# Cell 7 of an mLSTM, the last of its first full chunk, computed in turned form like the cells after it

## The chip, the core and the metric

The kernel runs on one core of one Trainium2 chip. Its engines work side by side and meet through semaphores: PE (TensorE, matrix products), DVE (VectorE), ACT (ScalarE), POOL (GpSimd) and SP (SyncE, which here issues nearly all transfers, in the order of its queue). The metric is the device time of one execution in microseconds (us). Three runs of the kernel before took 536.65, 540.45 and 540.67, the median is 540.45.

## The reference, cut to what matters

There are 4 batches and 8 heads, 768 tokens, head dimension 40. For every batch and head an mLSTM runs over the tokens:

```
m_new  = max(f + m, i);  fs = exp(f + m - m_new);  is = exp(i - m_new)
C      = fs * C + is * outer(v, k)
n      = fs * n + is * k
y      = sigmoid(o_gate) * (C q) / max(|n . q|, 1)
```

The result, 3072 tokens of 320 values (8 heads by 40), goes through a feed-forward block with 2048 inner units, `h = x @ w_in; out = (h * cos(h)) @ w_out`. Everything is float32.

## The kernel before

**Cells.** The sequence is cut in 6 chunks of 128 tokens. A cell is one chunk of one batch, all 8 heads; cell n = 4c + b is batch b of chunk c, so there are 24. Within a chunk the recurrence is written as products: the scores k q of all pairs of tokens (`scores`, L440), weighted with exponentials of the gates (`weigh`, L450, into the tile E), times the values; and what the chunks before left in the state `st[b]`, times q. The state is then faded and added to (`fade` L560, `seam` L569 and `state` L596). The value tile and the state carry one column more, from which n . q comes.

**Two forms of a cell.** Cells below `TURNED` (L70, here 8) take the plain form. q and k come as tokens by (head, dimension). PE transposes them (`turn`, L421, eight transposes for the four head pairs of q and k), ACT copies them out of PSUM (`turn_out`, L432). `values_kept` (L455) multiplies q with the state, and `values` (L466) the weights with the values; both give tokens by dimensions. `normalize` (L525) on DVE scales the state's part, adds, divides and applies the output gate. In `seam` PE transposes the result back in three blocks (L576), and `seam_out` (L590) copies it on ACT into `xT`, the input of the feed-forward block (dimensions by tokens).

Cells from `TURNED` on take the turned form. q and k are loaded in blocks (L319 to L325, eight transfers of 32 rows each), such that `turn_blocks` (L406) can turn them with DVE, one instruction for each of q and k (L412); the second half of that function scales q with the gate G, which `load_G` (L331) has spread over the rows (L415), and turns the output gate, loaded in blocks as well (L304 to L306), in two instructions (L419). `values_turned` (L475) computes dimensions by tokens at once: 16 products of the state with the scaled q (L484), 16 of the values with the weights (L490), each float32 product as two instructions. `normalize_turned` (L493) needs no transposes on PE: it works in place, writes the first 32 dimensions of each head into `xT` (L516), and sends the last 8 through a scratch in DRAM, two writes (L520) and two reads into `xT` (L523).

**Order.** The whole program is written out by hand, and every engine works through its own queue in that order. `first_cells` (L768) does the cells of chunk 0 and the first loads. Then `both_parts(c, b)` (L904) takes a quarter of the feed-forward block of chunk c together with cell n = 4(c + 1) + b, so that cell 7 lies in both_parts(0, 3) and its preparation at the end of both_parts(0, 2). A part runs: the up products of one eighth (class `Up`, L621 and L624 on PE), scores, then on ACT and DVE the steps near (L629), rest (L632), sin (L637) and gate (L641); the down products of the eighth before (`down`, L744, products at L754 while c = 0); the values and the normalizing of the cell; the second eighth likewise, with seam, state and weigh_k; its down products; and last the turning of the next cell. The PSUM pools are small: two banks for up products, two for the cells (`ps_a`), four for the down products.

While c = 0, the float weights are still being put together from raw bits: each piece is loaded into a tile `bits` (L129 for w_in, L170 for w_out, 8 pieces of w_out with three buffers), prepared on ACT (`parts`, L132), and joined on DVE and POOL (`join`, L143; POOL's addition is L149). Piece p of w_out serves down(c, p). The load of piece p + 3 stands in SP's queue where piece p is joined (`out_join`, L899), and it waits there until the buffer is read. Two pieces are joined in each part of c = 0, the second one after the turning of the next cell (L1014 to L1020). The output gates of chunk c + 2 are loaded in part (c, 2) (L975) and go through the sigmoid on ACT in part (c, 3) (L939); the weights E of cell n + 1 are prepared in part n (`decay_by_bias`, L383, while c = 0).

Of the kernel before, what the change touches and what calls it, by code (L numbers as in the profile page):

```python
# [29 lines left out]
def kernel(  # L30
# [22 lines left out]
    B, H, S, D = q.shape  # L53
# [13 lines left out]
    DA, DL, T4 = 32, 8, 4  # L67
    assert DM - NK * 128 == 64 and NF % 4 == 0 and DA + DL == D
    NB = 4
    TURNED = 2 * B  # L70
    SPREAD = (0, 1)

    const = ctx.enter_context(tc.tile_pool(name="const", bufs=1))
# [218 lines left out]
    def load_o(c, bs=range(B)):  # L292
        if c not in sig:
            sig[c] = p2.tile([128, B * DM + LO], FP, name="o", tag="o")
            if c > 1:
                nc.gpsimd.memset(sig[c][:, B * DM:], 0.0)
        for b in bs:
            o = sig[c][:, ts(b, DM)]
            if c * B < TURNED:
                nc.sync.dma_start(out=o.rearrange("t (h d) -> t h d", h=H),  # L300
                                  in_=o_gate[b, :, ts(c, C)].rearrange("h t d -> t h d"))
                continue

            for k4 in range(HP):  # L304
                nc.sync.dma_start(out=o[ts(k4, 32)].rearrange("r (i x) -> r i x", i=2),
                                  in_=o_gate[b, ts(k4, 2), ts(c, C)].rearrange("i (r x) d -> r i (x d)", x=T4))  # L306
# [5 lines left out]
    def blocks(n):  # L312
        return [qbs[n % 2 + i].rearrange("r (p x) -> r p x", p=HP) for i in (0, 2)]

    def load(n, which="qkv"):
        c, b = divmod(n, B)
        i = n % NB
        if n >= TURNED:
            for dst, src in zip(blocks(n), (q, k)):  # L319
# [42 lines left out]
    def psum_o():  # L362
        return ps_o.tile([128, HP, C], FP, name="pm", tag="o")
# [33 lines left out]
    def psum(n):  # L397

        return (ps_o, "o") if n < B and n % 2 == 1 else (ps_a, "a")
# [6 lines left out]
    def turn_blocks(n):  # L406


        c, b = divmod(n, B)
        qkT[n] = [p2.tile([128, HP, C], FP, name=f"t{i}", tag=f"t{i}") for i in range(2)]  # L410
        for dst, src in zip(qkT[n], blocks(n)):
            nc.vector.transpose(out=dst.rearrange("r p (t x) -> r p x t", x=T4),  # L412
                                in_=src.rearrange("r p (x d) -> r p x d", x=T4)[:, :, :, 0:32])
        qgs[n] = rooms[0][:, 0:HP * C].rearrange("r (p t) -> r p t", p=HP)
        nc.vector.tensor_tensor(out=qgs[n], in0=qkT[n][0], in1=Gs[n], op=OP.mult)  # L415
        oTs[n] = rooms[4][:, 0:4 * C].rearrange("r (i h t) -> r i h t", i=2, h=2)
        for half, lo in enumerate((0, LO)):
            o = sig[c][:, b * DM + lo:(b + 1) * DM + lo].rearrange("r (i x d) -> r i x d", i=2, x=T4)
            nc.vector.transpose(out=oTs[n][:, :, half].rearrange("r i (t x) -> r i x t", x=T4), in_=o[:, :, :, 0:32])  # L419
# [20 lines left out]
    def scores(n):  # L440
        pool, tag = psum(n)
        qT, kT = qkT[n]
        ps = [pool.tile([128, HP, C], FP, name="ps", tag=tag) for _ in range(2)]
        for p in range(HP):
            for j in range(2):
                r = slice(64 * j, 64 * j + (64 if n < TURNED else D))
                nc.tensor.matmul(ps[j][:, p], kT[r, p], qT[r, p], start=True, stop=True)  # L447
        pss[n] = ps

    def weigh(n):  # L450
        for j in range(2):
            w = Es[n].rearrange("p (a j) t -> p a j t", j=2)[:, :, j]
            nc.vector.tensor_tensor(out=w, in0=pss[n][j], in1=w, op=OP.mult)  # L453

    def values_kept(n):  # L455

        pool, tag = (ps_o, "o") if n == B else psum(n)
        heads_of[n] = None
        if n >= B:
            pq = pool.tile([128, H, D1], FP, name="pq", tag=tag)  # L460
            for p in range(HP):
                nc.tensor.matmul(pq[:, 2 * p:2 * p + 2].rearrange("p j d -> p (j d)"), qkT[n][0][:, p],
                                 st[n % B][:, p].rearrange("p j d -> p (j d)"), start=True, stop=True)
            heads_of[n] = pq
# [104 lines left out]
    def seam(n):  # L569

        pool, tag = psum(n)
        if n < TURNED:

# [78 lines left out]
    def parted(c):  # L652
        return c > 0
# [18 lines left out]
    def sums(c, f2):  # L672

        if not parted(c):
            return
        S = p2.tile([128, 4, C], FP, name="sg", tag="wt")
        A11, A21, A12, A22 = (gs[c, 2 * f2 + e][:, ts(b, C)] for e in range(2) for b in range(2))
        for i, (x, y, op) in enumerate(((A21, A22, OP.add), (S[:, 0], A11, OP.subtract),
                                        (A11, A21, OP.subtract), (A12, S[:, 1], OP.subtract))):
            nc.gpsimd.tensor_tensor(out=S[:, i], in0=x, in1=y, op=op)  # L680
        sg[c, f2] = S
# [81 lines left out]
    def warm(k, bank=None):  # L763

        for _ in range(k):
            nc.tensor.matmul(bank or pw, nil, nil.unsqueeze(1).to_broadcast([128, HP, 128]), start=True, stop=True)
# [128 lines left out]
    def out_parts():  # L895
        p, piece = outs.pop(0)
        return p, parts(*piece)
# [6 lines left out]
    def both_parts(c, b):  # L904

        n = (c + 1) * B + b
        cell = n < N  # L910
        begin = c == b == 0
        more = cell and n + 1 < N
        f2 = 2 * b
        up = Up(c, f2, cell_after_first if begin else None)
        if cell:
            scores(n)
            if begin:
                values_kept(n)

                warm(6, psum_o())  # L920
        for e in range(2):
            up.near(e)
        if begin:
            weigh(n)
        for e in range(2):
            up.rest(e)
        if cell and not begin:
            weigh(n)
        if begin or more and c > 0:
            decay_exponents(n + 1)  # L930
        for e in range(2):
            up.sin(e)
            up.gate(e)
        sums(c, f2)
        if c == 0 and b == 1:
            sigmoid(1, slice(1, B))
        if begin:
            sigmoid(1, slice(0, 1))
        if b == B - 1 and c + 2 < NC:  # L939
            sigmoid(c + 2)  # L940
        h = ()
        if c == 0 and not begin:
            out_join(*out_parts())
        if pieces:
            h = parts(*pieces.pop(0))
        rest = None
        if b == 0 and c > 0 and parted(c - 1):
            rest = down(c - 1, NF // 2 - 1)
        if begin or more and c > 0:
            decay(n + 1)  # L950
        elif more:
            decay_by_bias(n + 1)
        if f2 > 0:
            down(c, f2 - 1)
        elif rest:
            rest()
        elif c > 0:
            down(c - 1, NF // 2 - 1)
        if cell:
            if n + 2 < N:  # L960
                load(n + 2)
            if n < TURNED:
                if not begin:
                    values_kept(n)
                values(n)
                normalize(n)
            else:
                values_turned(n)
            if h:
                join(*h)  # L970
            if TURNED <= n + 2 < N:
                load_G(n + 2)
            if n + 3 < N:
                load_E(n + 3)
            if b == B - 2 and c + 2 < NC:  # L975
                load_o(c + 2)
            if n >= TURNED:
                normalize_turned(n)
            fade(n)
        h = ()  # L980
        sin_next()
        if pieces:
            h = parts(*pieces.pop(0))
        up = Up(c, f2 + 1)
        if cell:
            seam(n)
        for e in range(2):
            up.near(e)
        for e in range(2):
            up.rest(e)  # L990
        if cell and n < TURNED:
            seam_out(n)
        if h:
            join(*h)
        if cell:
            state(n)
        for e in range(2):
            up.sin(e)
            up.gate(e)
        sums(c, f2 + 1)  # L1000
        if more:
            weigh_k(n + 1)
        if c == 0 and b == B - 1 or c == 1 and b < B - 1:
            two_differences(c * (2 * b + 2))
        if pieces:
            join(*parts(*pieces.pop(0)))
        down(c, f2)
        if pieces:
            join(*parts(*pieces.pop(0)))
        if c == 0:  # L1010
            if b + 2 < B:
                pieces.extend(weights_in(b + 2))
            h = out_parts()
        if more and n + 1 < TURNED:  # L1014
            turn(n + 1)
            turn_out(n + 1, c > 0)
        elif more:
            turn_blocks(n + 1)
        if c == 0:
            out_join(*h)  # L1020

# [37 lines left out]
```

## Time and profile before

| what | us |
|---|---|
| median of three runs (536.65, 540.45, 540.67) | 540.45 |
| the profiled execution, its time | 537.82 |
| the profiled execution, its span (first to last instruction) | 536.1 |
| PE busy in the span | 524.8 |
| DVE, ACT, POOL busy | 365.7, 261.6, 168.0 |
| both_parts(0, 2), by its up products on PE | 83.42 to 106.78 |
| both_parts(0, 3) | 106.78 to 129.44 |
| both_parts(1, 0), first products | 129.44 |

Times inside the profile count from the span's start. A line of a timeline gives start, length, engine, source line and operation, the tile written and those read, the shape and how many instructions are merged; in brackets the idle time before it and what ended that. The chain of waits is followed back from the last instruction, at each step to what released it. "SPq L170" is the issue of a transfer by SP's queue at line 170. The granted clock of PE is 1.0 throughout.

### The profile page before, as it was taken

The numbers are of one execution on the slowest core, as the hardware profiler recorded it, in microseconds if no ns is written. First come the engines' busy times: TensorE is split into PE (matmuls) and PEld (weight loads), VectorE is DVE, ScalarE is ACT, GpSimd is POOL, SyncE is SP. The second block draws the span as 40 slices with busy tenths as digits, with TensorE's granted clock in tenths as the row PEclk, the third lists the DMA queues.
The fourth block names the chain that finished last, engine by engine and source line by source line (L and its number), as shares of the span: only waits on it lengthen the run. The fifth ranks groups of instructions, "written<-read, shape, count | busy, mean of one in ns | idle before, by whom it ended". The sixth has DMA issues, their size and how long they took to land.

```text
span 536.1 us, 9942 instructions
## 1 busy us (share of the span) xinstructions
PE 524.8 (98%) x3634; PEld 332.6 (62%) x3634; DVE 365.7 (68%) x727; ACT 261.6 (49%) x416; POOL 168.0 (31%) x304
## 2 busy tenths in 40 slices
PE   9888999999999999999999999999999999999997
PEld 6755666665565666666666656656656756656555
DVE  6778778868677677777767777767776765422323
ACT  4868696765633445543436525427335322332312
POOL 7512433516253453223322322422212221212121
PEclk9999999999999999999999999999999999999999
DMA  9989995952265752166743076635075000010001
GB/s 139 214 214 250 230 225 164 196 113 46 73 139 125 165 109 62 51 140 144 159 99 82 14 174 134 141 82 123 6 177 107 14 15 11 6 49 0 2 0 49
DMA packets 134513, 56.86 MB, mean 106 GB/s; under 512 B 72081, under 2 KB 130529, under 8 KB 134465
## 3 DMA queue, kind: packets, MB, share of 16 engines
q1 hardware_dynamic: 134320, 56.04, 47.1%
q8 instruction: 28, 0.46, 0.4%
q0 software_dynamic: 96, 0.18, 0.2%
q14 instruction: 21, 0.16, 0.1%
q10 hardware_dynamic: 48, 0.02, 0.0%
HBM read 50.00 MB, written 6.21 MB: 105 GB/s over the span
## 4 chain that ended last, share of the span: by engine, by line
PE 80%; SPq 6%; DMA 5%; DVE 4%; ACT 4%; issue 1%; POOL 1%; DVEq 0%; ACTq 0%; POOLq 0%
PE po L697 32%; PE pup L621 28%; PE pup L624 9%; PE hp L490 3%; PE ps L447 3%; PE po L754 3%; DMA E<-M_d 2%; SPq L329 2%; PE hp L484 2%; SPq L129 1%; PE pu L586 1%; DMA bits<-in_moe_w_in_dram 1%; SPq L300 1%; DMA qs<-in_q_dram 1%; DVE n L632 1%
## 5 line engine op out<-in xcount | busy, mean ns | idle before, releaser
L621 PE MATMUL pup<-xT,w_in_sb 128*128 128x512 f32 x384 | 175.0, 598 | 0.7 <-DVE g L641 0.3
L629 ACT ACTIVATE n<-pup 128x512 int32<-128x512 f32 x96 | 52.0, 593 | 211.7 <-PE pup L624 211.7
L632 DVE SCALAR_TENSOR_TENSOR n<-pup,n 128x512 f32<-128x512 f32 x96 | 61.9, 686 | 122.1 <-ACT n L629 122.1
L697 PE MATMUL po<-w_out_sb,g 128*128 128x320 f32 (+1 forms) x480 | 118.6, 396 | 0.0
L621 PEld LDWEIGHTS pup<-xT,w_in_sb 128*128 128x128 f32 x384 | 69.7, 190 | 72.8 <-issue 63.4
L697 PEld LDWEIGHTS po<-w_out_sb,g 128*128 128x128 f32 x480 | 83.5, 190 | 36.7 <-issue 9.1
L680 POOL TENSOR_TENSOR sg<-g 128x128 f32<-128x128 f32 x80 | 36.7, 458 | 192.4 <-DVE g L641 191.0
L637 ACT ACTIVATE n<-n 128x512 f32<-128x512 f32 x96 | 58.9, 630 | 12.1 <-DVE n L632 12.1
L641 DVE SCALAR_TENSOR_TENSOR g<-pup,n 128x512 f32<-128x512 f32 x96 | 61.7, 685 | 2.5 <-ACT n L637 1.2
L624 PE MATMUL pup<-xT,w_in_l 64*128 64x512 f32 x192 | 54.2, 641 | 2.2 <-DVE w_in_l L149 2.2
L373 POOL TENSOR_SCALAR_AFFINE_SELECT E<-E 128x1024 f32<-128x1024 f32 x19 | 20.8, 1093 | 102.0 <-DVE E L372 81.0
L697 PE MATMUL po<-T,sg 128*128 128x160 f32 x240 | 39.4, 300 | 0.0
L624 PEld LDWEIGHTS pup<-xT,w_in_l 64*128 64x128 f32 x192 | 14.4, 184 | 38.7 <-issue 35.6
L754 PE MATMUL po<-w_out_sb,g 128*128 128x320 f32 x128 | 36.6, 439 | 0.1
L697 PEld LDWEIGHTS po<-T,sg 128*128 128x128 f32 x240 | 34.8, 190 | 0.2
L412 DVE STREAM_TRANSPOSE t<-qs 128x512 f32<-128x512 f32 x32 | 32.7, 1101 | 0.0
L447 PEld LDWEIGHTS ps<-t,t 40*128 40x128 f32 (+1 forms) x384 | 25.1, 188 | 9.7 <-issue 9.4
L453 DVE TENSOR_TENSOR E<-ps,E 128x512 f32<-128x512 f32 x48 | 30.7, 681 | 0.4 <-PE ps L447 0.4
L381 ACT ACTIVATE E<-E 128x1024 f32<-128x1024 f32 x21 | 22.2, 1057 | 17.4 <-POOL E L373 16.2
L754 PEld LDWEIGHTS po<-w_out_sb,g 128*128 128x128 f32 x128 | 23.7, 190 | 9.7 <-POOL w_out_sb L149 0.3
L447 PE MATMUL ps<-t,t 40*128 40x128 f32 (+1 forms) x384 | 25.8, 274 | 0.0
L372 DVE TENSOR_TENSOR E<-E,tab 128x1024 f32<-128x1024 f32 x19 | 23.1, 1216 | 3.3 <-DMA E<-M_d 3.3
(152 smaller groups left out, 640.6 us busy)
## 6 DMA issues: line engine op xcount, KB each, us to landing
E<-M_d SPq DMA_DIRECT2D x22, 512.0 KB
bits<-in_moe_w_in_dram SPq DMA_DIRECT2D x40, 128.0 KB
bits<-in_moe_w_out_dram SPq DMA_DIRECT2D x8, 640.0 KB
room<-G_d SPq DMA_DIRECT2D x32, 128.0 KB
ks<-in_k_dram SPq DMA_DIRECT2D x24, 160.0 KB
vs<-in_v_dram SPq DMA_DIRECT2D x24, 160.0 KB
qs<-in_q_dram SPq DMA_DIRECT2D x32, 80.0 KB
qs<-in_k_dram SPq DMA_DIRECT2D x32, 80.0 KB
```

The lines of the kernel that those rows point to most:

```text
L412: nc.vector.transpose(out=dst.rearrange("r p (t x) -> r p x t", x=T4), in_=src.rearrange("r p (x d) -> r p x d", x=T4)[:, :, :, 0:32])
L447: nc.tensor.matmul(ps[j][:, p], kT[r, p], qT[r, p], start=True, stop=True)
L453: nc.vector.tensor_tensor(out=w, in0=pss[n][j], in1=w, op=OP.mult)
L621: nc.tensor.matmul(pu, w_in_sb[:, i, ts(block(f2, e), 128)], x(i), start=(i == 0), stop=False)
L624: nc.tensor.matmul(pu, w_in_l[r, f2], x(NK, r), start=False, stop=True)
L629: nc.scalar.activation(out=self.n[e], in_=self.pu[e], func=AF.Copy, bias=0.25)
L632: nc.vector.scalar_tensor_tensor(out=self.n[e].bitcast(FP), in0=self.pu[e], scalar=0.25, in1=self.n[e], op0=OP.add, op1=OP.subtract)
L637: nc.scalar.activation(out=r, in_=r, func=AF.Sin, scale=TWO_PI_DOWN)
L641: nc.vector.scalar_tensor_tensor(out=g, in0=self.pu[e], scalar=TWO_PI, in1=self.n[e].bitcast(FP), op0=OP.mult, op1=OP.mult)
L680: nc.gpsimd.tensor_tensor(out=S[:, i], in0=x, in1=y, op=op)
L697: nc.tensor.matmul(out, g, w, start=(f2 == 0 and first), stop=end, skip_group_check=True)
L754: nc.tensor.matmul(po[c][b], gs[c, f][:, ts(b, C)], w_out_sb[:, f], start=(f == 0), stop=(f == NF - 1))
```

## The change

`TURNED` becomes 7, so cell 7, batch 3 of chunk 1, is computed in the turned form. Its output gate (L304), its q and k (L319) and G (L972) are loaded in the forms that the turned cells use, and the 9 spare columns behind chunk 1's output gates are set to zero. `turn_blocks` is split: it keeps the turning of q and k, and the scaling of q and the turning of the output gate go into `turn_gates`. For the cells from 8 on both are called in one place as before. For cell 7 `turn_blocks` stands at the end of both_parts(0, 2), in place of `turn` and `turn_out`, and `turn_gates` in both_parts(0, 3) behind the gate step of the first eighth.

```diff
-    TURNED = 2 * B
+    TURNED = 2 * B - 1
...
             sig[c] = p2.tile([128, B * DM + LO], FP, name="o", tag="o")
-            if c > 1:
+            if (c + 1) * B > TURNED:
                 nc.gpsimd.memset(sig[c][:, B * DM:], 0.0)
         for b in bs:
             o = sig[c][:, ts(b, DM)]
-            if c * B < TURNED:
+            if c * B + b < TURNED:
                 nc.sync.dma_start(out=o.rearrange("t (h d) -> t h d", h=H),
                                   in_=o_gate[b, :, ts(c, C)].rearrange("h t d -> t h d"))
                 continue
...
     def turn_blocks(n):
-        c, b = divmod(n, B)
         qkT[n] = [p2.tile([128, HP, C], FP, name=f"t{i}", tag=f"t{i}") for i in range(2)]
         for dst, src in zip(qkT[n], blocks(n)):
             nc.vector.transpose(out=dst.rearrange("r p (t x) -> r p x t", x=T4),
                                 in_=src.rearrange("r p (x d) -> r p x d", x=T4)[:, :, :, 0:32])
+
+    def turn_gates(n):
+        c, b = divmod(n, B)
         qgs[n] = rooms[0][:, 0:HP * C].rearrange("r (p t) -> r p t", p=HP)
         nc.vector.tensor_tensor(out=qgs[n], in0=qkT[n][0], in1=Gs[n], op=OP.mult)
...
         sums(c, f2)
+        if n == TURNED:
+            turn_gates(n)
         if c == 0 and b == 1:
             sigmoid(1, slice(1, B))
...
         elif more:
             turn_blocks(n + 1)
+            if n + 1 > TURNED:
+                turn_gates(n + 1)
         if c == 0:
             out_join(*h)
```

## The prediction

> **What bounds the kernel now.** I read the page first, then the chain of waits around the cell, then the timelines of PE, SP, DVE and POOL from 84 to 136 us. The cell that changes, n = 7, is worked on in the two parts that stand at 82.6 to 129.4 us of the span: both_parts(0, 2) turns its q and k, both_parts(0, 3) does the rest. The page says TensorE:
>
> ```profile
> PE 524.8 (98%) x3634; PEld 332.6 (62%) x3634; DVE 365.7 (68%) x727; ACT 261.6 (49%) x416; POOL 168.0 (31%) x304
> ```
>
> That share is an average. The chain of waits, cut to this stretch, does not run through PE between 94 and 135 us:
>
> ```profile
> 92.42 0.41 DVE wt L144
> ...
> 93.38 0.84 DVE wt L148
> 94.22 0.02 SPq L170
> ...
> 94.27 0.38 SPq L170
> ...
> 111.61 3.36 DMA o<-in_o_gate_dram
> ...
> 115.06 1.28 ACT L310
> ...
> 120.29 2.45 ACT E L387 x8
> ...
> 124.25 0.49 ACT n L629
> ...
> 127.96 1.09 DVE t L412 x2
> ...
> 132.52 0.84 DVE wt L148
> ...
> 133.49 1.55 POOL w_out_sb L149
> 135.04 0.04 issue
> 135.09 4.57 PE po L754 x16
> ```
>
> Columns are start, length, what. Read it upwards from the last row: down(0, 7) at 135.09 waited for the last piece of w_out (p = 7) to be joined by POOL, that for VectorE, which did it after turning the blocks and gates of cell 8, that for the activation of the last up product (near, L629), that for ScalarE, busy without a gap since the sigmoid of chunk 2 at 115.06, that for the landing of chunk 2's output gates, and that for SP, which issues back to back from 94.27, when a buffer of `bits` came free. PE's own work beside this chain in the timeline (start, busy; the difference of two starts is what a group takes):
>
> ```profile
> 105.90 0.60 PE L428 MATMUL pt<-ident,qs 128*128 128x128 f32 x4
> ...
> 112.26 4.57 PE L754 MATMUL po<-w_out_sb,g 128*128 128x320 f32 x16
> 116.67 1.02 PE L462 MATMUL pq<-st,t 128*128 128x82 f32 x8
> 117.52 1.92 PE L472 MATMUL ph<-vs,E 128*128 128x41 f32 x16
> 119.26 3.68 PE L621 MATMUL pup<-xT,w_in_sb 128*128 128x512 f32 x8
> 122.87 1.13 PE L624 MATMUL pup<-xT,w_in_l 64*128 64x512 f32 x4
> 123.93 0.73 PE L576 MATMUL px<-ident,z 128*128 128x128 f32 x3
> ```
>
> PE and the chain run side by side: at 135 us PE had waited only 0.3 us for POOL. So what PE saves before 135.09 is lost there, if the chain is as late as now; what the chain loses is paid in full, beyond what PE still has to spare. After 135.09 PE goes on without a gap of note, and nothing there changes.
>
> **The change part by part.** All durations are from the profiled execution, whose span is 536.1 and whose time 537.82 (1.72 lies around the span); the median of the three runs is 540.45, 2.63 above it, and the runs go from 536.65 to 540.67. The sum is made against 537.82 and then put on the median.
>
> PE. Removed: turn(7), 105.90 to the next product at 106.78, 0.88; values_kept, 116.67 to 117.52, 0.85; values, to 119.26, 1.74; the transposes of the result, 123.93 to 124.59, 0.66: 4.13 us. Added: values_turned, as cell 8 does it at 139.59 to 141.20, 1.61. The scores over 40 rows instead of 64 take the same 1.06 (133.93 and 111.27). Net 2.52 us less.
>
> ScalarE. Three copies go (L434 0.58, L438 0.59, L594 0.45). The first two stand at 107.16 to 108.21, before 3.25 us idle; the third at 125.11, where the sine waits for VectorE anyway. Nothing.
>
> VectorE. turn_blocks(7) costs what cell 8's costs, 127.87 to 129.76, 1.89, and stands at the end of both_parts(0, 2) ahead of the join of w_out piece 5. That join ran at 107.25 to 109.53 and POOL's part of it at 109.68 to 111.21; down(0, 5), which needs it, began at 112.26 and would now be ready at 112.26 - 0.88 = 111.38. Moved by 1.89, POOL ends near 113.1, or near 112.7 if the 0.90 that L146 took there while POOL ran goes back to the 0.49 it took at 118.86. So down(0, 5) starts at 112.7 to 113.1: 1.3 to 1.7 of PE's saving is spent here at once. After it come 4.41 and 1.61 to the next up product, at 118.7 to 119.1, against 119.26 now. The near of that product did not wait for PE at 124.16, so up to 119.3 this costs nothing more.
>
> turn_gates(7) is 129.76 to 131.48, 1.72, after the gates of the first half (115.78 now; about 115.1 to 115.8). VectorE idles 2.55 us there until 118.33 (it waits for ScalarE's L138, behind the sigmoid), so it is covered; the scaled q is ready by 116.5 at the latest, values_turned starts at 117.1 at the earliest. normalize_turned(7) takes 3.0 (141.12 to 144.12) for the 4.15 of normalize(7) (120.13 to 124.28); the next work, L632, waits for ScalarE until 124.76. Nothing, up to 1.6 us of lengthening. The product pu must wait until hp is read (L513, about 122.5 if the start is 120.13); PE arrives there at 123.4 or later.
>
> A page of the Trainium skill speaks against the move: "VectorE: DVE Perf Modes", the section "Rules for kernel authors", says to transpose 128 by 128 on TensorE where PSUM will do, and to leave VectorE the blocks of 32. The row agrees: eight transposes took 0.88 us on PE, the blocks take 1.89 on VectorE. The section on the three transpose paths of that page gives 390 ns for one TensorE transpose; by it PE would save 8 x 0.39 = 3.1 instead of 0.88, an estimate. By neither does the end move, since the chain does not pass there.
>
> SP, and the queue behind each step. The gate of cell 7 is loaded in 4 issues (0.59 each, 9.39 / 16 in load_o(2)) for one (1.69, 5.06 / 3): +0.7 at 50 us. load(7) gets the eight block loads that load(8) has (94.71 to 99.10, 4.4) for one of q (0.55): +3.85 at 73 us. load_G(7), 1.55 as at 100.41, stands behind it. Sum +6.1 us ahead of weights_in(3) and of w_out pieces 6 and 7. What hides it: the wait of SP for VectorE's joins,
>
> ```profile
> SPq L170 <- DVE wt L148: 10.7, 3, 6.6
> ```
>
> of which 2.3 lie before piece 6 (87.22) and 6.6 before piece 7 (94.27): SP has 8.9 to spare at 85 us, so piece 6 goes out near 91.0 and piece 7 still at 94.27, and the chain keeps its time. The weights of w_in that come 6.1 later begin at about 84 us and are used by ScalarE at 91.97, 98.39 and 103.17. Bytes: 576 KB of blocks for 160 of q, 256 of G: 672 KB more, 2.7 us at the 246 GB/s of 72 to 80 us, against DMA shares of 0.78 and 0.35 in 80 to 88 and 88 to 96 (7 us free). Piece 6 could still be landing when piece 7 starts: piece 7's own took 94.27 to 98.78, so one issued at 91.0 is down by 95.5, at most 1.2 us of overlap. Price on the chain 0 to +1.2; I take +0.2, because the nearest row (share 0.35 at 88 to 96) shows the engines mostly idle there.
>
> Moved past SP: load_G(9) now waits for turn_gates(7) to have read its room; that ends by 117, its issue stood at 117.85. The four transfers of the result (writes 1.20, then reads 2.1 us after the writes and 1.26 long, as at 205.97 to 210.56) go out from about 122.9 to 127.5; SP's next transfer is at 141.03, so nothing queues behind them. Their reader is L624 of the next product at about 131.9; at 215.89 L624 did not wait for reads issued 5.3 us before, so at worst they are down at 132.8, and PE could bear 133.0.
>
> POOL. One memset of 0.11 us early; fade(7) waits for values_turned, which is over 5 us before POOL gets there (124.11). Nothing.
>
> The end. PE reaches the up product of chunk 1 at 128.3 to 128.8 (its PSUM is free when the gates end, 127.96), scores end at 134.2 or so, and down(0, 7) still waits for POOL until 135.04. The wait grows from 0.3 to about 1. What is late next is only that. Sum: PE -2.52, spent +2.52 in the waits before down(0, 5) and down(0, 7), chain +0.2: 537.82 + 0.2 = 538.0, on the median 540.6.
>
> **Rivals.**
> - The saving arrives. It needs the chain to be 2.5 us earlier, as it would be if the sigmoid at 115.06 did not wait for its transfer, or if piece 7 were joined before the blocks. For it: PE is 98% busy. Against: the order in VectorE's queue and the load of the gates stay. 537.82 - 2.5 = 535.3, on the median 537.9.
> - SP is late, the side of slower. Place: piece 6 and 7 of w_out behind the added issues. It decides when piece 6 goes out after 93.9, that is when the early delay is over 9.0 us and not 6.1, or when the added bytes hold piece 7's landing; past that every us moves the gates of chunk 2, the sigmoid and down(0, 7). If the cover is gone, all 6.1: 543.9, on the median 546.6. Against: 8.9 us of wait in SP's queue.
> - VectorE's order costs more. If the join of piece 5 ends after 113.3 (L412 and the join stretched beside POOL), near and all behind it slip by the excess. The row: L146 took 0.90 beside POOL and 0.49 alone; three instructions stretched by 0.41 add 1.2 to the 112.7 to 113.1 above. Price at most about 1 us: 538.8, on the median 541.6. [...]
>
> **How the numbers follow.** No change of note 0.74, the saving arrives 0.10, VectorE's order 0.08, SP late 0.08. The likeliest gives 540.6. Low 535.9: 537.9 less about half the spread of the runs shown (4.02). High 543.6: 540.6, plus the 1.0 left of the bound on landing, plus half the spread. About 1% (5.4 us) is what a measurement of this kernel can tell from no change. Faster by over 1% would need twice what PE saves: 0.04. Slower by over 1% is SP late with all its 6.1 us and little more: 0.08. Within: 0.88.
>
> **What would show it.** Right: L462 and L576 one group fewer; PE idle before L754, released by POOL's L149, in two places: 1.3 to 1.7 us near 111.4 and about 1 us near 134; SP's wait before L170 near 87 gone and the one before 94.27 cut to about 3; L310 again at 115; down(0, 7) at 135.1 to 135.5. Wrong: down(0, 7) before 134 (the chain was shorter than I read it), or L310 after 116.5 (SP was late), or PE waiting for qgs before L484 or for X_d before L624.

## The result, and the profile after

The changed kernel takes 538.88 us, the kernel before 540.14 (medians of 20 runs each; 537.05 to 541.13 and 536.65 to 541.53). The ratio is 0.9989 with an interval of 0.9971 to 1.0007: no difference that the times can show. The profiled execution has a span of 535.3 us for 536.1.

The runs of one kernel scatter by 4 to 6 us, and most of that scatter comes ahead of the change, before 50 us of the span (last section). So the profiles are compared by a stretch that excludes it: from PE's first up product of part (0, 2) to the start of down(0, 7). What follows, from down(0, 7) to the end, took 401.0 us in 13 of the 14 profiles of this case and 400.8 in one.

| kernel (first profile; second) | stretch, us | sigmoid of chunk 2 begins, us after the stretch's start | PE's waits in the stretch |
|---|---|---|---|
| before | 51.66; 51.35 | 31.64; 30.64 | 0.3 before down(0, 7); none |
| changed | 51.01; 50.96 | 30.07; 29.78 | 1.27 and 0.43; 1.29 and 0.44 (before down(0, 5), down(0, 7)) |

PE has become shorter by what was said, and waits in the two places that were named. PE's timeline of the changed kernel (lines stand 3 lower than before: L757 is down, L624 and L627 are up, L450 the scores, L487 and L493 values_turned):

```profile
105.89 3.60 PE L624 MATMUL pup<-xT,w_in_sb 128*128 128x512 f32 x8
109.42 1.13 PE L627 MATMUL pup<-xT,w_in_l 64*128 64x512 f32 x4
110.38 1.06 PE L450 MATMUL ps<-t,t 40*128 40x128 f32 x16
112.71 4.57 PE L757 MATMUL po<-w_out_sb,g 128*128 128x320 f32 x16 [1.27 <-POOL w_out_sb L149]
117.22 0.67 PE L487 MATMUL hp<-room,st 40*32 40x128 f32 x32
117.81 1.08 PE L493 MATMUL hp<-E,vs 128*32 128x128 f32 x32
118.83 3.70 PE L624 MATMUL pup<-xT,w_in_sb 128*128 128x512 f32 x8
122.46 1.13 PE L627 MATMUL pup<-xT,w_in_l 64*128 64x512 f32 x4
...
134.34 4.57 PE L757 MATMUL po<-w_out_sb,g 128*128 128x320 f32 x16 [0.43 <-POOL w_out_sb L149]
```

The transposes between the down products and L624 at 105.89 are gone, values_turned takes 117.22 to 118.83 = 1.61, and both waits are for POOL's L149, which puts a piece of w_out together. The first of them is VectorE's order: blocks, then the join (timelines of DVE and POOL):

```profile
107.23 2.03 DVE L411 STREAM_TRANSPOSE t<-qs 128x512 f32<-128x512 f32 x2
109.10 0.48 DVE L144 TENSOR_SCALAR wt<-wt 128x640 f32<-128x640 f32 x1
109.62 0.50 DVE L146 TENSOR_SCALAR wt<-wt 128x640 int32<-128x640 int32 x1
110.15 0.82 DVE L148 SCALAR_TENSOR_TENSOR wt<-bits,wt 128x640 int32<-128x640 int32 x1
```

```profile
111.12 1.54 POOL L149 TENSOR_TENSOR w_out_sb<-wt,wm 128x640 int32<-128x640 int32 x1 [2.93 <-DVE wt L148]
```

The chain of waits is the part that did not stay. In the kernel before it came from SP through the gates' landing and the sigmoid. Now the sigmoid begins at 113.40, not at 115.06, ScalarE is done early, and near (L632) waits for PE:

```profile
113.40 1.28 ACT L310 ACT_TABLE_LOAD   x1 [0.24 <-DMA o<-in_o_gate_dram]
...
123.62 1.08 ACT L632 ACTIVATE n<-pup 128x512 int32<-128x512 f32 x2 [1.01 <-PE pup L627]
```

Between the join and down(0, 7) the chain now runs through PE and VectorE (chain of waits of the changed kernel: start, length, what):

```profile
107.31 1.95 DVE t L411 x2
...
111.12 1.55 POOL w_out_sb L149
112.67 0.04 issue
112.71 4.57 PE po L757 x16
...
122.53 1.11 PE pup L627 x4
123.64 0.59 ACT n L632
...
127.44 1.09 DVE t L411 x2
...
131.78 0.84 DVE wt L148
...
132.75 1.54 POOL w_out_sb L149
134.30 0.04 issue
134.34 4.57 PE po L757 x16
```

SP did what was reckoned. Before w_out piece 7 it waited 4.1 us for VectorE's join in place of 6.6, and issued it at the same time:

```profile
SPq L170 <- DVE wt L148: 5.1, 2, 4.1
```

### The profile page after: what moved, and what is told of

It reads as the page before. It is cut to its first block, busy times and chain, and to the rows that moved or that the text cites. A ratio compares the mean times of both kernels' runs of the same rounds, so it can differ in the third digit from the quotient of the medians.

```text
span 535.3 us, 10028 instructions
## 1 busy us (share of the span) xinstructions
PE 522.5 (98%) x3663; PEld 329.9 (62%) x3663; DVE 368.9 (69%) x734; ACT 260.5 (49%) x413; POOL 167.8 (31%) x305
## 4 chain that ended last, share of the span: by engine, by line
PE 82%; SPq 5%; DMA 4%; DVE 4%; ACT 2%; issue 1%; POOL 1%; DVEq 0%; POOLq 0%; ACTq 0%
PE po L700 32%; PE pup L624 28%; PE pup L627 9%; PE po L757 3%; PE hp L493 3%; PE ps L450 3%; SPq L329 2%; PE hp L487 2%; DMA bits<-in_moe_w_in_dram 1%; DMA E<-M_d 1%; SPq L129 1%; PE pu L589 1%; DMA qs<-in_q_dram 1%; DVE wt L148 1%; SPq L300 1%
## 5 line engine op out<-in xcount | busy, mean ns | idle before, releaser
L624 PE MATMUL pup<-xT,w_in_sb 128*128 128x512 f32 x384 | 175.1, 598 | 0.7 <-DVE g L644 0.3
L632 ACT ACTIVATE n<-pup 128x512 int32<-128x512 f32 x96 | 52.0, 593 | 212.5 <-PE pup L627 212.5
L635 DVE SCALAR_TENSOR_TENSOR n<-pup,n 128x512 f32<-128x512 f32 x96 | 61.9, 686 | 119.9 <-ACT n L632 119.9
L624 PEld LDWEIGHTS pup<-xT,w_in_sb 128*128 128x128 f32 x384 | 69.7, 190 | 73.2 <-issue 63.4
L627 PE MATMUL pup<-xT,w_in_l 64*128 64x512 f32 x192 | 54.2, 641 | 2.0 <-DVE w_in_l L149 2.0
L757 PE MATMUL po<-w_out_sb,g 128*128 128x320 f32 x128 | 36.6, 439 | 1.7 <-POOL w_out_sb L149 1.7
L627 PEld LDWEIGHTS pup<-xT,w_in_l 64*128 64x128 f32 x192 | 14.4, 184 | 38.5 <-issue 35.6
L411 DVE STREAM_TRANSPOSE t<-qs 128x512 f32<-128x512 f32 x34 | 34.7, 1098 | 0.0
L450 PEld LDWEIGHTS ps<-t,t 40*128 40x128 f32 (+1 forms) x384 | 25.1, 188 | 9.7 <-issue 9.4
L456 DVE TENSOR_TENSOR E<-ps,E 128x512 f32<-128x512 f32 x48 | 30.7, 681 | 0.4 <-PE ps L450 0.4
L757 PEld LDWEIGHTS po<-w_out_sb,g 128*128 128x128 f32 x128 | 23.7, 190 | 11.4 <-POOL w_out_sb L149 2.1
L450 PE MATMUL ps<-t,t 40*128 40x128 f32 (+1 forms) x384 | 25.8, 274 | 0.0
```

Of the source, the lines that this page charges most:

```text
L624: nc.tensor.matmul(pu, w_in_sb[:, i, ts(block(f2, e), 128)], x(i), start=(i == 0), stop=False)
L627: nc.tensor.matmul(pu, w_in_l[r, f2], x(NK, r), start=False, stop=True)
L632: nc.scalar.activation(out=self.n[e], in_=self.pu[e], func=AF.Copy, bias=0.25)
L635: nc.vector.scalar_tensor_tensor(out=self.n[e].bitcast(FP), in0=self.pu[e], scalar=0.25, in1=self.n[e], op0=OP.add, op1=OP.subtract)
L757: nc.tensor.matmul(po[c][b], gs[c, f][:, ts(b, C)], w_out_sb[:, f], start=(f == 0), stop=(f == NF - 1))
```

## The experiments

Four questions: is PE's saving real, which order holds it back, how much can SP's queue still bear, and what does a longer wait of PE cost? All kernels compute the whole of it. Two load scraps of 64 bytes besides, into a room that is free then and filled properly later; two turn a block twice; one adds products on zeros.

**1. The join of piece 5 ahead of cell 7's blocks.**

```diff
+        if n + 1 == TURNED:
+            out_join(*h)
         ...
             turn_blocks(n + 1)
         ...
-        if c == 0:
+        if c == 0 and not (n + 1 == TURNED):
             out_join(*h)
```

> The changed kernel with the join of w_out piece 5 put ahead of the turning of cell 7's blocks (at the end of part (0, 2) only). Theory A: VectorE is the scarce engine between 106 and 112 us; the join ends first, but the blocks then end near 111.4 while PE wants them for the scores at 110.4, so the 1.27 us wait before down(0, 5) goes and a wait of about 1.0 us before the scores comes in its place; down(0, 7) at 134.0 to 134.4 (134.34 now), span 535.0 to 535.3, time within 0.1% of the changed kernel's. Theory B: the order of the two steps alone costs the 1.27 us: no wait in either place, down(0, 7) near 133.3, span 534.3.

Measured: stretch 51.00, ratio to the kernel before 0.9995 (0.9971 to 1.0018). PE's waits in this profile:

```profile
PE ps L450 <- DVE t L411: 1.1, 1, 1.1
PE po L757 <- POOL w_out_sb L149: 0.4, 1, 0.4
```

The wait has moved from the down products to the scores, and down(0, 5) starts no earlier (29.37 us after the stretch's start, 29.38 in the changed kernel): theory A. VectorE has 3.75 us of work there (blocks and join, 107.23 to 110.98); PE wants the blocks at 110.4 and the piece, 1.5 us of POOL later, at 111.4. An exchange of the two steps saves nothing.

**2. The kernel before with the join of piece 7 ahead of cell 8's blocks and gates.**

```diff
         elif more:
+            if c == 0:
+                out_join(*h)
             turn_blocks(n + 1)
-        if c == 0:
+        if c == 0 and n + 1 < TURNED:
             out_join(*h)
```

> The kernel before with the join of w_out piece 7 put ahead of the turning of cell 8's blocks and gates (end of part (0, 3)). Theory A: PE's own work ended only 0.2 to 0.3 us before that join in the kernel before, so PE and the chain ran side by side: the wait before down(0, 7) goes, down(0, 7) at 134.8 to 134.95 for 135.09, span 535.8 to 536.0, time the same. Theory B, that the kernel before lost more than that to the chain: down(0, 7) before 134, time faster by over 0.2%.

Measured: stretch 51.38, no wait, down(0, 7) at 134.81; ratio 0.9976 (0.9947 to 1.0006). Theory A, but the sigmoid also began 0.9 us earlier than in the first profile before, so this profile does not show the edit alone: the kernel before without it has no wait either in its second profile (51.35, sigmoid 1.0 earlier). The 0.3 by which the first profile is longer is made of two delays: the transposes of the result took 0.66 for 0.48, and down(0, 7) began 1.16 after the scores for 1.03 (0.99 here). So PE and the chain came out together, as was read, and the chain cost the kernel before 0.3 at most.

**3. Sixteen more issues in SP's queue.**

```diff
                 load_G(n + 2)
+                if n + 2 == TURNED:
+                    for i in range(16):
+                        nc.sync.dma_start(out=rooms[1][0:16, i:i + 1], in_=fg[0:16, i:i + 1])
```

> The changed kernel with 16 more transfers of 64 bytes issued by SP behind load_G(7), into a room that is free there and is filled properly later: about 6.4 us more in SP's queue and no bytes to speak of. Theory A: SP had 4.1 us left before w_out piece 7 (the wait of its issue for VectorE), so its issue moves from 94.26 to about 96.5, the output gates of chunk 2 land about 2.2 us later, the sigmoid starts at 115.6 to 117.2 instead of 113.4 and down(0, 7) at 135.5 to 137.1 instead of 134.34; span 536.5 to 538. Theory B, SP's queue has nothing to do with the end: span 535.3, sigmoid where it was or hidden.

Measured: stretch 57.24, 6.2 more than the changed kernel; ratio 1.0108 (1.0066 to 1.0150). Theory A in kind, but two to five times its size (down(0, 7) was to move by 1.2 to 2.8). The 16 issues took 7.56 us. Piece 7 went out at 96.7, as expected, but it was not the first thing to miss its time: the pieces of w_in (L129), which SP issues between the added transfers and L170, began at 88.87 instead of 82.82. ScalarE's waits in this profile:

```profile
ACT wt L138 <- DMA bits<-in_moe_w_in_dram: 4.9, 1, 4.9
...
ACT L310 <- DMA o<-in_o_gate_dram: 2.3, 1, 2.3
```

For a piece of w_in ScalarE waited 4.9 us, its join then held the up products of part (0, 3), and after that the clock fell (below). The gates of chunk 2 were late as well, the path that theory A had named, and the normalizing and the last join behind them. PE's waits:

```profile
PE pup L624 <- POOL w_in_sb L149: 3.4, 1, 3.4
PE pu L589 <- DVE room L516: 1.4, 1, 1.4
PE po L757 <- POOL w_out_sb L149: 1.4, 1, 1.4
```

Together 6.2, and 1.7 for the clock, in place of the 1.7 that the changed kernel waits: the 6.2 of the stretch.

**4. Four more issues**, the same edit with `range(4)`.

> The changed kernel with 4 more 64-byte transfers behind load_G(7), about 1.9 us of SP's queue. From the run with 16: there the first late thing was not piece 7 of w_out but a piece of w_in, for which ScalarE waited 4.93 us when the issue was 6.1 us later in the span and 6.8 later against PE, so the changed kernel has about 1.9 us to spare there. Theory A (that reading): nothing moves by more than 0.3 us, stretch 50.9 to 51.4. Theory B, that the changed kernel already stands at the edge: ScalarE waits 1.5 us or more for that piece and the stretch grows to 52.5 or more.

Measured (one execution): stretch 50.95, span 534.2, and no wait of ScalarE for the pieces of w_in: theory A. So after the change SP's queue still bears 4 issues more there (they took 1.99 us), and not 16. By the shift of run 3 (issues 6.1 us later in the span, 6.8 against PE, for a wait of 4.9) the changed kernel has about 1.9 us to spare there, an estimate.

**5. Cell 7's blocks turned twice.**

```diff
-        for dst, src in zip(qkT[n], blocks(n)):
+        for dst, src in list(zip(qkT[n], blocks(n))) * (2 if n == TURNED else 1):
```

> The changed kernel with the two turning instructions of cell 7's blocks issued twice. Theory A: the chain to the end runs through VectorE at 107 us: the join of piece 5 ends 1.88 us later, PE waits 3.15 instead of 1.27 us before down(0, 5), and down(0, 7) starts 1.9 us later, at 136.2, span 537.2. Theory B: the chain through ScalarE (sigmoid, near) sets the end and has slack: PE's wait grows by 1.88, but down(0, 7) moves by less than 0.9 us, span below 536.2.

Measured: stretch 54.47, 3.46 more than the changed kernel; ratio 1.0043 (1.0022 to 1.0063). There is no slack behind this place (theory A, not B), and 1.6 us came on top. PE waited 0.69 before the scores and 2.14 before down(0, 5), where 3.15 had been expected in one wait. PE's timeline shows where the 1.6 went: down(0, 5) took 6.13 us from start to start, for 4.51.

```profile
114.87 6.21 PE L757 MATMUL po<-w_out_sb,g 128*128 128x320 f32 x16 [2.14 <-POOL w_out_sb L149]
121.00 0.67 PE L487 MATMUL hp<-room,st 40*32 40x128 f32 x32
```

**6. One block more**, the first of the two instructions twice (`zip` list with its first pair ahead of it).

> The changed kernel with one of the two turning instructions of cell 7's blocks issued twice: 0.94 us more on VectorE ahead of the join of piece 5. Theory A: the wait before down(0, 5) grows from 1.27 to 2.2 us and down(0, 7) moves by 0.9, stretch 51.9, if PE's granted clock stays at 1.0; with a stretch of 0.5 of 3.4 us as after the wait of the doubled run, 1.7 more: 53.6. Theory B, slack on the way: stretch below 51.4.

Measured (one execution): stretch 53.77, that is 2.76 more than the changed kernel: 0.9 from VectorE and 1.7 from the clock, as the second half of theory A had it. The wait was 2.15 us, and down(0, 5) took 6.20.

**7. Cell 7's blocks a part earlier**, behind the join at the end of part (0, 1).

```diff
-        elif more:
+        elif more and n + 1 > TURNED:
             turn_blocks(n + 1)
-            if n + 1 > TURNED:
-                turn_gates(n + 1)
+            turn_gates(n + 1)
         if c == 0:
             out_join(*h)
+        if n + 2 == TURNED:
+            turn_blocks(n + 2)
```

> The changed kernel with turn_blocks(7) a whole part earlier, at the end of part (0, 1) behind the join there, where VectorE idles 1.58 us before L635; everything else as in the changed kernel. The meter is the stretch from PE's first up product of part (0, 2) to down(0, 7): 51.66 us before, 51.01 changed. Theory A: the wait before down(0, 5) goes (1.27 us) without one before the scores, but down(0, 7) still waits for the join of piece 7, which hangs on near, and near on PE (now 1.0 us after ScalarE is free) or on ScalarE: stretch 50.0 if the sigmoid starts as early as in the changed kernel's profile, up to 51.6 if it starts as late as in the profile before. Theory B: the wait before down(0, 5) was the whole loss: stretch 49.3 whatever the sigmoid does.

Measured: stretch 50.28; ratio 0.9974 (0.9944 to 1.0005). No wait before the scores or down(0, 5). Before down(0, 7) PE waited 1.09, and near did not wait for PE, with the sigmoid 30.22 after the stretch's start: theory A. Of the 1.27 that were freed, 0.7 arrived.

**8 and 9. The same with the join of piece 7 ahead of cell 8's blocks and gates**, taken twice, on two chips.

```diff
         if c == 0:
             out_join(*h)
+        if more and n + 1 > TURNED:
+            turn_blocks(n + 1)
+            turn_gates(n + 1)
         if n + 2 == TURNED:
             turn_blocks(n + 2)
```

> As the run with the blocks early, and also the join of w_out piece 7 ahead of the turning of cell 8's blocks and gates. Theory A: both waits before down products go; PE's saving of 2.5 us arrives nearly whole, stretch 49.2 to 49.4 (50.2 if the sigmoid is late, by the PSUM of the up products), span about 533.6, time 0.3 to 0.5% below the kernel before. Theory B, the saving on PE is not real time (its products overlap with others or the clock takes it back): stretch over 50.5.

> Both joins first, once more, for its time: stretch 49.1, time ratio 0.995 to 0.998 of the kernel before.

Measured: stretch 49.10 and 50.16; ratios 0.9980 (0.9959 to 1.0001) and 0.9971 (0.9947 to 0.9994); medians 538.29 for 540.01 of the kernel before, and 536.42 for 537.98. In the first profile PE waits nowhere in the stretch, which is 2.25 shorter than the second profile of the kernel before: PE's saving is real. In the second profile ScalarE waited 1.84 us for the gates, the sigmoid began 31.6 after the stretch's start, the normalizing of cell 7 was late behind it, and the product pu waited for it:

```profile
123.01 0.51 PE L589 MATMUL pu<-vs,kw 128*40 128x41 f32 x16 [0.99 <-DVE room L516]
```

That is 1.0 of the 1.06 by which the two profiles differ. The 49.1 expected of it was missed; 50.2 is what had been expected of the first run for a late sigmoid, though by PSUM and not by this product. The interval of run 9 lies clear of no change; that of run 8, on the other chip, reaches it.

**10. PE's early wait filled**, on top of 8.

```diff
+        warm(6)
         values(1)
```

> As both joins first, with six products on zeros (warm) put ahead of values(1), where PE waits 1.8 us for v at 24 us of the span and where five of the eight profiles so far show a granted clock of 0.5 for 10 to 17 us soon after or a stretch of it elsewhere below 50 us. Theory A: that wait lets the clock fall, and the fall is the scatter of the times; filled, the clock stays at 1.0 from 20 to 60 us, part (0, 2) starts on PE at 83 to 84 us in the profile, and the median is under 537 with a smaller spread. Theory B: the clock falls whatever PE does there: the median as in both joins first (538), spread 3 us or more.

Measured: stretch 49.10, part (0, 2) from 84.41, median 536.09 for 537.98; ratio 0.9974 (0.9947 to 1.0002). Inconclusive: the fill stood one cell too early, as the product that waits for v at 24 us is that of values(2). The wait did not show in this profile, since PE came there later, and the clock was 1.00 from 20 to 40 us; from 40 to 60 it was 0.91, behind a wait of 2.33 for a piece of w_in. Of the ten profiles taken by then, four have 10 to 17 us at half clock below 50 us and four have stretches of 3.4. Eight of twelve times lie between 535.88 and 536.22, but two are above 540, and run 9 on the same chip has 536.42 without the fill.

**11 and 12. Both kernels once more.**

> The kernel before once more, for how far its own profile moves: stretch 51.66 give or take 0.2; the sigmoid of chunk 2 starts between 113.4 and 115.1.

> The changed kernel once more: stretch 51.0 give or take 0.2, waits before down(0, 5) and down(0, 7) of 1.27 and 0.43; if the sigmoid starts near 115 as in the profile before, up to 0.7 more.

Measured: stretch 51.35 and 50.96, as in the table: the kernel before 0.3 lower than it was (within 0.2 was expected), the changed one as it was, with the sigmoid early again. Spans 539.9 and 538.1: both were 3 to 4 us late at the start of the stretch already.

## Why the prediction was right, and the step that was not

- No change that the times show: right, 538.88 for 540.14, with 540.6 forecast. The number alone says little: the range, 535.9 to 543.6, is nearly twice as wide as the scatter of the three runs before, and it holds the 537.9 of the rival in which all of PE's saving arrives. What decides between the two are the waits. By the stretch the change saves 0.65 in the first profiles and 0.39 in the second, where the sum had 0.2 more.
- PE's sum, 2.52 less: the rows of the second profile before give 0.87 + 0.85 + 1.75 + 0.48 - 1.61 = 2.34, since the 0.66 of the result's transposes in the first was a slow one. 2.25 of it arrive in run 8. The 0.09 between is a term that the sum left out: from down(0, 5) to the next product it is 4.50 with values_turned behind it, and 4.41 with values_kept (4.41 was used).
- The wait before down(0, 5), 1.3 to 1.7 with a start at 112.7 to 113.1: 1.27, at 112.71. L146 took 0.50 with POOL idle, the lower of the two ends.
- The wait before down(0, 7), about 1 us behind an unmoved chain through the sigmoid, "L310 again at 115", down(0, 7) at 135.1 to 135.5: this step of the prediction failed. The wait measured 0.43, L310 began at 113.40, down(0, 7) at 134.34, and ScalarE was free 1.0 us before PE's up product. The landing of chunk 2's gates was taken as fixed by SP's queue; the last issue moved by only 0.3 us, but ScalarE was released 1.7 earlier. Over the profiles with no added work in a queue the sigmoid began 29.8 to 31.6 us after the stretch's start, and the first profile was at the late end. One profile's wait for a transfer is one draw. Where the gates do land in time, the sigmoid starts when ScalarE has finished the sine before it, and the sine follows PE's up products, which come 0.9 earlier without turn(7). The second profiles show it, before and changed, with no idle time ahead of L310:

```profile
116.95 1.23 ACT L637 ACTIVATE n<-n 128x512 f32<-128x512 f32 x2 [0.27 <-DVE n L632]
118.19 1.28 ACT L310 ACT_TABLE_LOAD   x1
```

```profile
114.64 1.23 ACT L640 ACTIVATE n<-n 128x512 f32<-128x512 f32 x2 [0.27 <-DVE n L635]
115.89 1.28 ACT L310 ACT_TABLE_LOAD   x1
```

That is 30.6 and 29.8 us after the stretch's start (30.7 in run 2, 29.8 in runs 4, 8 and 10). So ScalarE's work from the sigmoid on hangs on PE too, which the prediction did not reckon with. In both profiles of the changed kernel the near, the gates, the turning of cell 8 and the join of piece 7 follow PE from down(0, 5) on, and not the sigmoid. With the sigmoid as late as in the first profile (31.6, near at 40.7 after the start for 40.3) the wait would have been about 0.9, an estimate: the forecast of 1 holds for a late landing only.

- turn_gates covered, the scaled q in time, the result's transfers in time: right. L487 did not wait, and L627 at 131.89 did not wait for the reads issued at 125.90. normalize_turned(7) took 4.4 (118.74 to 123.14) and not 3.0, most of the 1.6 of lengthening that was allowed; it began 1.4 before the old one, and L635 behind it waited 1.1 for ScalarE.
- SP: piece 7 at 94.27, wait of about 3 left: 94.26 and 4.1. But the reserve of 8.9 us counted only the waits of L170. The pieces of w_in behind the added issues had less, 6.1 + 1.9 = 8.0 by the estimate from run 3, and the rival's price of one to one was too low: 6.8 of delay, 1.9 of it covered, cost 6.2, of which the clock took 1.7.
- VectorE's order as a rival: it did not come about (the piece was ready at 112.67, the point of decision was 113.3). Its price of about 1 us was too low: in run 6, 0.94 us more on VectorE cost 2.8, of which the clock took 1.7. (Its 538.8 is 541.4 on the median, with the 2.63 added, and not 541.6.)

## What to carry to other kernels

Work taken off a busy engine arrives only if what it waits for next comes earlier too: here VectorE's queue held two joins that PE needed right behind the shortened parts, and 2.3 us of PE shrank to 0.4 to 0.7. To collect it, move the added work to where its new engine idles (the end of the part before), and put what others wait for ahead of what they do not; exchanging two steps inside a full stretch only moves the wait. Before trusting a chain through a transfer, take the profile twice, see what would set the time if the transfer came early, and compare stretches and not spans.

## What the runs showed of the hardware

**Waits of PE of 2.1 us were followed by a half clock for 3.4 us.** The granted clock in the profiles is 1.0 or 0.5. In run 5 (windows of 4 us; the third number from the end of a row is the granted clock, the two behind it are the DMA share and GB/s):

```profile
108.00:112.00 4.00, 3.31 (x16) 1.28 (x16) 3.97 (x6) 1.09 (x2) 0.51 (x1) 1.00 0.40 84
112.00:116.00 4.00, 1.86 (x16) 1.37 (x13) 3.97 (x7) 2.22 (x3) 1.54 (x1) 0.85 0.49 119
116.00:120.00 4.00, 4.00 (x12) 2.65 (x11) 3.93 (x8) 3.97 (x5) 0.00 (x0) 0.73 0.79 152
120.00:124.00 4.00, 4.00 (x71) 2.30 (x71) 1.55 (x5) 3.97 (x10) 2.77 (x3) 1.00 0.81 189
```

The loss of 0.15 and 0.27 of 4 us is a half clock for (0.60 + 1.08) / 0.5 = 3.4 us. Waits of 2.14 (with 0.69 shortly before), 2.15 and 3.4 us (runs 5, 6 and 3) were each followed by such a stretch, waits of 1.0 to 1.4 in the same part of the kernel never. It is not certain, and 2.1 is no threshold. In the first profile before, PE waited 2.24 us ahead of L624 at 42 us, and the clock stayed at 1.0; in run 10 it waited 2.33 at the same place, and the clock fell. At 14 us of the span waits of 0.7 to 1.1 were followed by a half clock in runs 1 to 5 and 9 (run 4, after 0.69: 0.57 from 16 to 20 us). What besides the length of the wait decides is not shown. The Trainium skill's page "TensorE: Matmul & The Clock Gate", section "Part 1: The HAM clock gate", gives a window of about 3.4 us and an idle window as the condition; the length agrees, but here the clock fell behind a wait of 2.1 us in run 6, and behind one of 0.7 in run 4.

**Most of the scatter of the times goes with this clock, ahead of the change.** In the kernel before the clock was 1.0 from 20 to 60 us in the first profile. In the second, after a wait of 1.81 us for v at 24 us (1.76 in the first), it was not:

```profile
20.00:40.00 20.00, 18.19 (x135) 15.00 (x134) 11.97 (x31) 12.09 (x21) 5.05 (x6) 0.64 0.90 208
40.00:60.00 20.00, 19.68 (x121) 11.78 (x121) 15.55 (x29) 16.99 (x27) 6.60 (x7) 0.93 1.04 234
```

By the same column that is (7.2 + 1.4) / 0.5 = 17 us at half clock. PE began the stretch at 87.55 instead of 83.42, and the span was 539.9 instead of 536.1. Over all profiles the start of the stretch goes from 82.5 to 87.6: in the five with 10 to 17 us at half clock below 50 us it is 85.0 or more, in the other nine 84.7 or less. The times agree: of 72 executions of the kernel before on three chips, the 28 with a mean clock of 0.987 or less took 539.3 to 542.1 us, the 31 with 0.996 or more 536.1 to 539.3. What decides in one execution whether the clock falls there stays open, and so does what moves the landing of chunk 2's gates by 1.8 us.
